# A searched order of 1,300 operations, searched again with GpSimd's casts kept apart from VectorE's on-chip operations

## The chip, the cores and the metric

The kernel runs on one core of one Trainium2 chip. The metric is the device time of one execution in microseconds. The inputs lie in HBM as float32 and the output goes there as float32. Inside, most operands are float16 and the sums in PSUM are float32.

## What is computed

The reference is a recurrence with decay for each head (B = 4 batches, H = 8 heads, S = 768 steps, D = 64), and then a mixer on its output, seen as 768 tokens by 512 channels for each batch:

```
gamma = 1.0 - 2.0 ** (-5.0 - np.arange(H))
scale = 1.0 / np.sqrt(D)
for t in range(S):
    state = gamma * state + einsum('bhd,bhe->bhde', k[:, :, t], v[:, :, t])
    y[:, :, t] = scale * einsum('bhd,bhde->bhe', q[:, :, t], state)
x = y.transpose(0, 2, 1, 3).reshape(B, S, H * D)

xt = x.transpose(0, 2, 1)
h  = maximum(xt @ w_tok1, 0) @ w_tok2        # 768 -> 256 -> 768 over the tokens
u  = x + h.transpose(0, 2, 1)
h2 = maximum(u @ w_ch1, 0) @ w_ch2           # 512 -> 1536 -> 512 over the channels
out = u + h2
```

## The kernel before

**The work and its stages.** The sequence is cut in six chunks of 128 steps. Two heads of 64 make a pair of 128 rows, so a batch has four pairs; "(2,1)" below is pair 1 of batch 2. `front(b, p)` is the work of one pair: 

- its k, q and v are loaded (`load`, L269). For batches 0 and 1 GpSimd's queue does that, and the transfer converts to float16 on its way; the very first k and all loads of batches 2 and 3 are issued on SP and arrive as float32 in tiles called `row` (L282).
- k is scaled by the decay of its step, one operation for each head (L343 on ScalarE or L345 on VectorE). For q the decay is either put in while its transpose is taken out of PSUM (L387, by the table `gq`), or with the same L343 and L345.
- where v came as float32, it is cast (L358 ScalarE, L360 VectorE or GpSimd). Six of those eight casts are GpSimd's, and besides issuing transfers and making two index tables at the start these are all that it does.
- k and q are turned so that a head's 64 dimensions lie on the partitions: by TensorE and a copy out of PSUM (L377, L379, L392), or, for batches 2 and 3 and some of batch 1, by a transposing transfer that SP issues (L367).
- "state matmuls" (L408) make each chunk's k times v; VectorE adds them up over the chunks with their decay (the chain of U, L418 and L420), and L434 or L436 writes them as the blocks of `diag`.
- "scores" (L453) are k times q inside a chunk, masked on VectorE (L463) into `am`. L474 and L483 give y from `am` with v and from `diag` with q.
- y is copied out as float16 `x` (L489), and the token mixer follows (L503 with its relu L512 or L514, and L523). Its result is cast to float16 `u` (L529) and copied to float32 `X` (L539), the sum onto which the channel mixer is added. u is turned too, on SP (L553) or on TensorE (L568, copied out at L575).

`back(b)` is the channel mixer of one batch: the widening 512 to 1536 (L606 with its relu L622; batches 2 and 3 use a scheme of seven products for eight, L679 to L725), and the narrowing 1536 to 512, also with seven products (operand sums L784, products L820 and L830, banks kept aside L810, additions to X L837, output L862). The last three blocks of batch 3 use plain products (L746, L755, L761). The schemes need sums and differences of weights, `wsum` (L904, L917), made once by VectorE.

**What sets the order.** Every operation is an `Op` in a list, with the engines that may do it. No planner runs in the kernel: a string, PLAN (L40 to L70), names the operations one by one in the order in which they are to be emitted. Two characters are an operation's number; one more says which engine does it, where there is a choice, and one more which of the eight PSUM banks it takes. A "+" with a digit stands for that many spare matmuls, zero times zero into bank 7, which keep TensorE from standing idle (L935, here called fillers). The loop that emits them:

```
    for step in placed(ops, PLAN):
        if isinstance(step, int):
            ...
            for _ in range(step):
                nc.tensor.matmul(spare[:, :384], zero[:, :P], zero, start=True, stop=True)
        else:
            step[1][3]()
```

Each engine, and each queue of transfers, takes its own instructions in that order and waits at each until what it reads is there and what it overwrites has been read. So an instruction whose input is late holds up all that stands behind it on its engine. Tiles of one name share a few buffers: `row` and `v` have four each, kT three, qT four, `diag` three, `am` six. A load into a buffer waits for the last reader of what the buffer held.

**The start.** Before the first pair, VectorE writes small tables: the logarithms of the decays `lgs` (L198 to L200), `lnh` (L219), the decay of a chunk `gp` (L229, L230), the mask, and zeros for `diag` (L233). From them ScalarE makes gk and gy (L204, L205), the scales of k and of q, and the table `gq` with four exponentials (L224). GpSimd issues the loads of batches 0 and 1 and of all weights, in one queue.

Of the kernel before, what the change touches and what calls it, by code (L numbers as in the profile page):

```python
# [39 lines left out]
PLAN = (  # L40
    "000b09010704020f0d1h00a031i10506+e1n0+31l11o1j20e1p081m1q0c1W31X1k0+31w121A1v451r1x1S0+42x30g1T1+21U41V0+42642"
    "1y0h0k1s2y1z0i2730292t11B51Y11t01Z1E61u02b2u00j201C281F2v21D0212w0+42H242a2c0222J232z32K1G02A240+12I212501H41I"
    "2L2d0m1J02f22g0l2B2M2C2e03812h02D2E390n0p2Q43413511N2i32F02G02j1K2k02N12O0r2P12l2R1L01O01M13630E2o3a72m03712T5"
    "2S02n01P00q2U3b2p03c3d3e2V03i033L61Q53k3f2q03g03j023l3h03n3m0u0o2W2X02Z0t3M2r33o20s3p2Y03013r00v3q03s4k13H13t0"
    "3I11R03u63v2s13w04l3273J53300x3x3A3N70w5s33y03D13B03F3z10z0yaC23C0aF03G13E0aDbc1bdbe5taEbf33O3K0bg3P3Qbl6bh311"
    "3R4g13S4h1aGbi2bmaHbn3V57413W3Y4m33Z0A3T04nbjaL0aMbk4i4aI2aNaJ4300F3X4074j04o3U1aK4u4156bA2410D0C0B4p444q4wbB"
    "4x4rbCb91b05b1421451b32ba4634P0b24Q14y474804v4T64V44cbJ3494a0bKb44s14Ubb4b0bL1d4W4X4R6b54YaU54S14C1aO7aP5o04d0"
    "aQbr3b624z6b74Z1f504t1b8bsaX74f4e14AaV4B0aR24DaS0G511aY521btaW535304aTaZbx21e4F74E154570Kby0I5p0bM4G4H0bu4bG5"
    "bvbo7bw565q04IbzbHbD25r0bNbO550H4J015bEbS0bQ31716bPbFbIbp0R5b55c602582bq59c8184Lcc7bR1bT5a05d04K05e45f5g1620"
    "4M04N01b631cd00L5Y0ce6bX0bY5Z0bV5hbW0c9cb5u15i065466bZch640J4O617M16A2cf67c005v5j07N0ci0685wcac4c1695x5k5yc25z"  # L50
    "5l0cl5m0cu5C10266a0N5Dcv5Ecy5cA4cj1cB0M6b0cm06C05A0cz1c5cq5F5H4cD5B05I6c0cE05Gcr6d62306gck5K75J05LcH5M05N36D0"
    "5O6hcn5P05Q5ncwcx0S0Q5R06f6l3c36ecI15TcF26m5U0cG5W6cM5X15V06EcN6y16i76j6z0dL6cJdq5cK5S1cocZ0dMdU27K16BdVdrcQ1"
    "dscRd84dNdW781cL19d96k1d00Pdk26F6790cS0OdR5dS6G6H6Id16n06JbU6K6o06p1ada1ccT46q0dO10T6L1dPcU6rdl7I17c0dQdT6s07b"
    "6t1d51dm7d16M07a2d6dw56N72066ud76Qdb16O6Rdcdd7J00VdX0dYdZ6P6v17edF76V18i1dn2dxdycV6W7O7f07g7P6dG6S56T8j0dHdo"
    "dh46U0di7hcg7icW77j6X07k6Y07Q7R6Z7Sdp7Ldz27l07008m1cpdjdAdB6w1cX717217T0U731cY74de2dfdg7n7340dt5du7U7p750d22d3"
    "7r7o8n06xdv760d47qdI07X75367v4e07s20X7V081e2e17m0dC18k2807YdD7t7wdJdE7W17u07x0dKeb67y1eIeJeK7Z1geceL7z850e470W"
    "7A08U00Ye507E7Be617C07F0e9cs18258o8S1eO3e38T0cCef837G07D0868Z2eg8l8W18p4ea0908qed7He79112840eM68818reP8s870e8"
    "89ee0ei8X18t92938a08e8ueh8beN08c08VeT177eU8d094ej8f0eRemeQes5eS0eteVen8x72438zeq5eo8h8Yc61eXeW09w08B11ct113er0"
    "8v08y9x00Z10a428AeYf0f19u2evew0f4epex7f5ey8w0ezf86cP08g0eueA0c708C18D970432989bf9eBfc8F08GeCfm28E0999aeD8I7f6"
    "fdcO08H0eEfa3fb8J950eFf7eZfnfo48K0961fffgfe78LfqfD5fh9c3fkfrfpfEa218M0ftfH9dfifAfja319y8N0fl9s19t19f49g9v149e0"  # L60
    "f219h08Ofu8P0fs68R9i18Q1fv9jfF79k0fy9lfGa90aa9z1fz9o9A9m0fIabfw9Bac9C9p09q0gm7fx9DadfKfJ2gnfR4fLgqfP9Eae9n0fS"
    "f319H0316fCfM9L9KfVfNfQg85fT69F0go1fO9Ja5grfWgtfX2fYgpfU9Ig9gs1gugcfZgvg09G0ge6ga0gbg5g39M3gAgdg6gfgy9Na60gggh"
    "9P09O09Qg1g2gwgxg79R0gkgigja709S29TgCfB9U0glgzg4gDgH19Y9VgI19W0gJ5gBgFgKgEaf0gZh34a89Z09X0gO7h0ah3526ajala1ai"
    "h40gMel09rh8gN0eH0gPh1akgQa01h90hcag0am3anha6ao0ap2gGhd1as0aqek0ar0gR1gSgVhbh2heathhau0avaw0hlgThmhfayhnh56az0"
    "hoh6h7hghp0hHax0hr3hw6hq0gWhxgLhuhZ1aBhshv0gUhAhL3i0ig7hyhIhMhti3hN5hihBgX0hz0hPhChKhDi4i6hOihhQhF0hJiki16ii5"
    "iu4hSi2ijidi7i56hR5ibhEhTilhUi8hXinhVicaA0hYiL0im1hWi9j55ioisipiaiviZ3ieiw2itiqiMirixiyizj17j0iN6iPgY0iBj3iQj4"
    "iIiOj2iR2iA6iSk67iCiDeG1jdiTj6j7iGjY1j8iJjbiXiUjeiHiEiYjcifjCj9jG4jEjajZk7k8iViFhj1hk1iWiKk0jfjgjN5k9jk2kahG0"
    "k1kbk2k3jDjOjRke6jH0jLjM0jijr3k4kckd1jPjFjl0jhjSk50jpjq0jI5jQ1jTjW1jsjJjtjvjjjKjwju0jm5jxjUjnjVjojykfkgkhjA0"
    "jX0kijzjB0kjkkkl0"
)  # L70


# [895 lines left out]
```

## Time and profile before

| | us |
|---|---|
| three runs | 188.21, 188.58, 189.45 |
| their median | 188.58 |
| the profiled execution: its own time | 188.52 |
| the profiled execution: its span, first to last instruction | 186.7 |
| VectorE busy | 167.7 |
| ScalarE busy | 122.1 |
| GpSimd busy | 33.6 |
| bytes moved | 30.23 MB |

The span is what the profile shows, and 188.52 - 186.7 = 1.82 us of the execution's time lie around it. Times inside the span are counted from its start. A row of a timeline reads: start, duration, engine, line, operation, output and input, shape, and how many like it follow in one go. Behind it, in brackets, stands how long the engine had been idle and whose result ended that. In a row that groups instructions, "x6 | 2.5, 415 | 0.9" means six of them, 2.5 us busy, 415 ns each on average, 0.9 us idle before them. "PE" is TensorE's matmuls, "DVE" VectorE, "ACT" ScalarE, "POOL" GpSimd, "SP" the engine that only issues transfers. The TensorE clock was granted in full in all 40 slices.

### The profile page before, as it was taken

Reading aid. Unit: us, or ns where it says so; the run is one execution under the profiler, and the core shown is the slowest. Engines: PE = TensorE matmul, PEld = TensorE weight load, DVE = VectorE, ACT = ScalarE, POOL = GpSimd, SP = SyncE. Lnnn points to the kernel's source line nnn. Section 1 sums busy time; section 2 is a strip of 40 time slices with the busy share of each in tenths; the row PEclk is TensorE's granted clock in tenths of the full one; section 3 lists DMA queues with packets and bytes.
Section 4 is the critical chain, followed back from the end, with each engine's and each line's share of the span. In section 5 each row is a group of like instructions: output and inputs, shape, how many; then the busy total and the mean of one; then the engine's idle time right before and its main releaser. Section 6 shows DMA issues by size and latency. Waiting matters only on the chain.

```text
span 186.7 us, 5207 instructions
## 1 busy us (share of the span) xinstructions
PE 178.8 (96%) x2075; PEld 134.9 (72%) x2075; DVE 167.7 (90%) x434; ACT 122.1 (65%) x279; POOL 33.6 (18%) x44
## 2 busy tenths in 40 slices
PE   7888999999999899999999999999999999999992
PEld 3445988677679779765768888776588986566782
DVE  3799998899999799889889999999999999879982
ACT  3837998856779676287988667689875254882110
POOL 8995676420001010001010000021000000000000
PEclk9999999999999999999999999999999999999999
DMA  8999999999999999999999959997926344011025
GB/s 113 154 171 195 178 176 178 185 187 205 190 183 217 183 230 167 148 226 205 131 228 234 162 101 215 312 192 171 157 42 146 111 140 185 2 58 58 32 112 197
DMA packets 94233, 30.23 MB, mean 162 GB/s; under 512 B 84352, under 2 KB 91264, under 8 KB 94208
## 3 DMA queue, kind: packets, MB, share of 16 engines
q1 hardware_dynamic: 61840, 17.63, 53.6%
q0 software_dynamic: 30208, 8.46, 43.8%
q10 hardware_dynamic: 2160, 3.80, 5.6%
q8 instruction: 16, 0.26, 0.6%
q14 instruction: 9, 0.07, 0.1%
HBM read 26.74 MB, written 6.29 MB: 177 GB/s over the span
## 4 chain that ended last, share of the span: by engine, by line
PE 59%; DVE 25%; DMA 6%; ACT 6%; issue 2%; POOL 0%; DVEq 0%; POOLq 0%; ACTq 0%
PE bank L606 15%; PE bank L820 9%; PE bank L679 9%; PE bank L830 7%; DVE am L463 5%; DVE X L837 4%; DMA row<-in_q_dram 4%; PE bank L503 4%; PE bank L523 3%; DVE U L420 3%; DVE hs L784 3%; PE bank L746 3%; DVE h L696 3%; DMA v<-in_v_dram 2%; PE bank L453 2%
## 5 line engine op out<-in xcount | busy, mean ns | idle before, releaser
L606 PE MATMUL bank<-uT,wc 128*128 128x384 f16 x192 | 36.4, 326 | 0.0
L463 DVE TENSOR_TENSOR am<-bank,mask 128x384 f16<-128x384 f32 x64 | 33.4, 552 | 1.5 <-PE bank L453 1.4
L622 ACT ACTIVATE h<-bank 128x384 f16<-128x384 f32 x48 | 22.0, 500 | 10.0 <-PE bank L606 9.8
L606 PEld LDWEIGHTS <-wc 128*128 128x128 f16 x192 | 17.3, 98 | 9.1 <-issue 0.2
L696 DVE TENSOR_TENSOR h<-bank,us 128x384 f16<-128x384 f32 x36 | 18.8, 553 | 2.0 <-ACT us L691 1.0
L691 ACT COPY us<-bank 128x384 f32<-128x384 f32 x36 | 16.6, 484 | 6.1 <-PE bank L679 2.2
L820 PEld LDWEIGHTS <-hs 128*128 128x128 f16 x198 | 18.8, 98 | 2.5
L810 ACT COPY us<-bank 128x256 f32<-128x256 f32 x26 | 9.6, 374 | 16.2 <-PE bank L820 13.8
L360 POOL CAST v<-row 128x768 f16<-128x768 f32 x6 | 5.0, 826 | 82.9 <-DMA row<-in_v_dram 53.6
L837 DVE TENSOR_TENSOR X<-X,bank 128x256 f32<-128x256 f32 x44 | 17.9, 417 | 1.0 <-PE bank L830 0.9
L420 DVE SCALAR_TENSOR_TENSOR U<-U,gp,bank 128x64 f32<-128x64 f32 x64 | 16.8, 278 | 0.8
L820 PE MATMUL bank<-wsum,hs 128*128 128x256 f16 x132 | 17.2, 273 | 0.0
L529 ACT CAST u<-bank 128x384 f16<-128x384 f32 x29 | 13.7, 491 | 4.1 <-PE bank L523 3.4
L679 PE MATMUL bank<-hs,wsum 128*128 128x384 f16 x72 | 15.1, 326 | 0.1
L434 ACT ACTIVATE diag<-U,gp 64x320 f16<-64x320 f32 x24 | 13.3, 559 | 2.6 <-DVE U L420 2.3
L523 PE MATMUL bank<-h,wt 128*128 128x128 f16 x192 | 14.8, 219 | 0.0
L489 ACT CAST x<-bank 128x384 f16<-128x384 f32 x27 | 12.2, 488 | 3.0 <-PE bank L483 2.9
L503 PE MATMUL bank<-x,wt 128*128 128x128 f16 x192 | 13.8, 219 | 0.2 <-DVE U L418 0.2
L830 PEld LDWEIGHTS <-h 128*128 128x128 f16 x132 | 12.5, 98 | 1.9
L679 PEld LDWEIGHTS <-wsum 128*128 128x128 f16 x96 | 9.1, 98 | 5.7 <-issue 0.4
L503 PEld LDWEIGHTS <-wt 128*128 128x128 f16 x192 | 11.9, 98 | 1.9 <-DMA wt<-in_moe_w_tok_dram 0.4
L523 PEld LDWEIGHTS <-wt 128*128 128x128 f16 x192 | 12.1, 98 | 1.2
(91 smaller groups left out, 364.4 us busy)
## 6 DMA issues: line engine op xcount, KB each, us to landing
out_dram<-X ACTq DMA_DIRECT2D x14, 256.0 KB, 2.3
row<-in_q_dram SPq DMA_DIRECT2D x8, 384.0 KB, 4.9
row<-in_v_dram SPq DMA_DIRECT2D x8, 384.0 KB, 5.1
row<-in_k_dram SPq DMA_DIRECT2D x8, 384.0 KB, 5.5
wc<-in_moe_w_ch_dram POOLq DMA_DIRECT2D x5, 512.0 KB, 13.3
out_dram<-X SPq DMA_DIRECT2D x9, 256.0 KB, 3.2
v<-in_v_dram POOLq DMA_DIRECT2D x8, 192.0 KB, 9.3
row<-in_q_dram POOLq DMA_DIRECT2D x8, 192.0 KB, 8.6
```

Source lines behind the costliest of these rows:

```text
L420: nc.vector.scalar_tensor_tensor(out=u[:, c], in0=u[:, c - 1], scalar=gp[:, p:p + 1], in1=st, op0=ALU.mult, op1=ALU.add)
L463: nc.vector.tensor_tensor(am, SC[g].tile[:, :m * P].rearrange("p (i t) -> p i t", t=P), mask.to_broadcast([P, m, P]), ALU.mult)
L503: nc.tensor.matmul(acc[:, jt * P:(jt + 1) * P], wt1[:, i, jt * P:(jt + 1) * P], X16.tile[:, i], start=(i + jt == 0), stop=(i == NC - 1), s ...
L523: nc.tensor.matmul(Y[hf].tile[:, i * P:(i + 1) * P], wt2[:, jt, t], H1.tile[:, jt], start=False, stop=(jt == NJ - 1), skip_group_check=True)
L606: nc.tensor.matmul(acc[:, :SH], wc1[:, ct, ft * P:(ft + 1) * P], UT.tile[:, ct, sh * SH:(sh + 1) * SH], start=(ct == 0), stop=(ct == NP - 1))
L622: nc.scalar.activation(H2.tile[:, ft], A.tile[:, :SH], AF.Relu)
L679: nc.tensor.matmul(acc[:, :SH], left(ct), r[:, ct], start=first and ct == 0, stop=ct == 1, skip_group_check=True)
L691: (nc.scalar.copy if e == "ACT" else nc.vector.tensor_copy)(kept(j), A.tile[:, :SH])
L696: nc.vector.tensor_tensor(into(hf)[:, ft], bank.tile[:, :SH], kept(j), ALU.add)
L820: nc.tensor.matmul(acc_[:, lo], l[:, j], r[:, j], start=first and j == 0, stop=j == K2 - 1, skip_group_check=True)
L830: nc.tensor.matmul(acc_[:, lo], l[:, j], r[:, j], start=first and j == 0, stop=j == K2 - 1, skip_group_check=True)
L837: (nc.vector if e == "DVE" else nc.gpsimd).tensor_tensor(dst(), dst(), b_(), ALU.add)
```

## The change

Only the table PLAN differs: another order, another choice of engine and of bank for the same operations, 38 fillers in place of 35. It comes out of a search that takes a cast on GpSimd and an on-chip operation of VectorE (one that reads and writes SBUF and no PSUM) to exclude each other, and that takes the time at which the early loads land from a trace. The first and last lines of the table:

```
 PLAN = (
-    "000b09010704020f0d1h00a031i10506+e1n0+31l11o1j20e1p081m1q0c1W31X1k0+31w121A1v451r1x1S0+42x30g1T1+21U41V0+42642"
...
+    "070504000b0102060f1h0031i108+g1n01j10d0a1o1p1q0e1l2+21W31k11m1v210h1S0091r1T01x1y0c1s+61B11U21X1w041A0g1V01Y5"
...
+    "jojX0kjjA0jzkkjB0kl0"
 )
```

What this does to the engines' own orders is shown at three places. The numbers behind a name (`k_115`, `bank_177`) only tell tiles apart.

At the start, ScalarE's order before. `us` is the buffer in which the first k, that of pair (0,0), lands:

```order
L204 ACT_TABLE_LOAD
L204 ACTIVATE gk<-lgs 128x8
L205 ACTIVATE gy<-lgs,lnsc 128x8
L343 ACTIVATE k_115<-us,gk 128x6x64
L224 ACTIVATE gq<-us,lnsc,lnh 128x384 x4
L392 COPY kT<-bank_177 128x768
L343 ACTIVATE k_233<-row,gk 128x6x64
L392 COPY kT<-bank_256 128x768
```

And now:

```order
L204 ACT_TABLE_LOAD
L204 ACTIVATE gk<-lgs 128x8
L205 ACTIVATE gy<-lgs,lnsc 128x8
L224 ACTIVATE gq<-us,lnsc,lnh 128x384 x4
L343 ACTIVATE k_124<-us,gk 128x6x64
L343 ACTIVATE k_215<-row,gk 128x6x64 x2
L392 COPY kT<-bank_240 128x768
L434 ACTIVATE diag<-U,gp 64x5x64 x2
```

The four exponentials go ahead of the first decay of k, the first copy of a turned k goes to VectorE, and both halves of the second pair's decay are ScalarE's.

SP's order where the loads of batch 2 begin, some 55 us into the execution, before:

```order
L553 DMA_TRANSPOSE uT<-u_1040 128x6x128
L282 DMA row<-in_q_dram 128x12x64
L282 DMA row<-in_v_dram 128x12x64
L282 DMA row<-in_k_dram 128x12x64
L282 DMA row<-in_q_dram 128x12x64 x2
L367 DMA_TRANSPOSE qT<-q_1317 128x6x128
L282 DMA row<-in_v_dram 128x12x64
L553 DMA_TRANSPOSE uT<-u_1229 128x6x128
L367 DMA_TRANSPOSE kT<-k_1327 128x6x128
```

And now:

```order
L553 DMA_TRANSPOSE uT<-u_1059 128x6x128
L282 DMA row<-in_v_dram 128x12x64
L282 DMA row<-in_k_dram 128x12x64
L282 DMA row<-in_q_dram 128x12x64
L282 DMA row<-in_v_dram 128x12x64
L282 DMA row<-in_q_dram 128x12x64
L282 DMA row<-in_k_dram 128x12x64
L367 DMA_TRANSPOSE kT<-k_1262 128x6x128
L367 DMA_TRANSPOSE qT<-q_1324 128x6x128
```

The first three loads are those of pair (2,0), q, v, k before and v, k, q now. The two q behind them were those of (2,3) and (2,1); now v, q and k of (2,1) follow, and q of (2,3) comes later.

VectorE's order at the same place, before. `q_1317` is q of pair (2,0), `q_1405` that of (2,3):

```order
L345 TENSOR_SCALAR q_1317<-row,gy 128x6x64
L837 TENSOR_TENSOR X<-X,bank_1336 128x256
L784 TENSOR_TENSOR hs<-hs,h_814 128x768
L784 TENSOR_TENSOR hs<-h_814,hs 128x768
L418 COPY U<-bank_1373 128x64
L345 TENSOR_SCALAR q_1405<-row,gy 128x6x64
L837 TENSOR_TENSOR X<-X,bank_1329 128x256
L420 SCALAR_TENSOR_TENSOR U<-U,gp,bank_1373 128x64
L418 COPY U<-bank_1360 128x64
```

And now, where `k_1262` is k of pair (2,0), in row 111 of VectorE's order:

```order
L904 TENSOR_TENSOR wsum<-wc_81 128x1536
L784 TENSOR_TENSOR hs<-hs,h_798 128x768
L784 TENSOR_TENSOR hs<-h_798 128x768
L345 TENSOR_SCALAR k_1262<-row,gk 128x6x64
L837 TENSOR_TENSOR X<-X,bank_1300 128x256
L784 TENSOR_TENSOR hs<-h_798,hs 128x768
L784 TENSOR_TENSOR hs<-h_821 128x768
L418 COPY U<-bank_1330 128x64
L418 COPY U<-bank_1341 128x64
```

One half of the k of (2,0) now stands ahead of the U copies, and no q does.

Over the whole execution these instructions change engine. ScalarE: L343 from 23 to 25, L358 from 1 to 2, L392 from 6 to 4, L434 from 24 to 25, L489 from 27 to 30, L512 from 15 to 14, L529 from 29 to 27, L539 from 22 to 25, L575 from 3 to none, L810 from 26 to 29, its output transfers (L862) from 13 to 11. VectorE: L345 from 25 to 23, L360 from 1 to none, L392 from 2 to 4, L436 from 8 to 7, L489 from 5 to 2, L514 from 1 to 2, L529 from 3 to 5, L539 from 10 to 7, L575 from 3 to 6, L810 from 7 to 4. GpSimd keeps six casts, with the v of pair (2,3) in place of that of (2,1).

More of the change, by code (lines that the diff above doesn't have):

```diff
@@ L40 @@
 PLAN = (
[L41 to L69, printed above, removed]
+    "070504000b0102060f1h0031i108+g1n01j10d0a1o1p1q0e1l2+21W31k11m1v210h1S0091r1T01x1y0c1s+61B11U21X1w041A0g1V01Y5"
+    "1Z+126231t02021274629221z1u0+71E02t02b1C1F2a280i0j2x62u02z32v4232A2y2B2C2D2E2f20k2w0+42H641D02401G02502K2J"
@@ new lines @@
+    "+23850m1H32F02c42d1I392G11J02N62g2I351K0l2L2M2e02h01N1L02i32O2j0n1M02Q11O02k00p3413511P00q2R3652l2m03a02P1371"
+    "3i533b2o2S03c3d3e3l0E2n02p02T72U2q03f3k0u3L43j233m2V02Z2W3n1Q53H13g03h03o23p0o1R12X03003r33s3112Y12r73253q00r"
+    "0s2s13313t00t0x3I03u03v5s63w05t3N73x0v3y03A3B03z03J53K0aF03M3D63FaC23E13C0aDaG0A3G1bc6aE3Obd3V2354aHbe3P3Q4g1"
+    "4k04h1bf64lbi1bgbjbh3R3S3ZbkaL00w3Y4i6bl4bm4j13WaM3XbG5bH4u26174xbn4m34w4n4340z3T0bIb953U04o0y4vba401bD64p4144"
+    "bbbJ5420aI2bEaNbF450aU0bKaVaX64q1b4rbL4s11f4P04y0F4t14Q11daR3aSaT46747aW4T34800C0D4V0aY49aJaZ4a04R74W4U4XaK5o0"
@@ new lines @@
+    "6t0dC30OdDdrds0N6ubU7M17N16v1cJcKdL1dEcodMdA6w1dN7c07d0dB0S6N25346R6P6F66GcQ17edb7cRd25dk0dw46Od3dxdy6H6I6Q7a2"
+    "6V3dldR2cScp6JcZ40V6K781d51d6d06L06S6d4dm6M16T7911adS6Wd1dU46U06X0dc6Y0dT6Z7K2d77P27010T7Q7f10W7gcT5cL7R7S7h71"
+    "7207bcU7Odt0730ddducV7i74751dn68i17j1gdh7do8j17TdvdpcW0cXcY7Ld85de6d98m07617kda7U8S1dfdidjdg7n52137r0Ye08T17o"
+    "7q7pe40e1dF6dGdHdVdWe507V0e3e20UdX3dI70XdY7X14657Z8l817l1dJe9dZea08n08odO37s2dPe647Y11dQ7W0dKe7edeb37m0eI7v4"
+    "eM77t7w8218W0ee0ei7u07y56x7x0eJeLecef83eN07zeK1c80cCej8VcP1eRemeg8X18U0850en868407A08k27BeS08Z38p5908q7E8708r"
@@ new lines @@
+    "gygga60ge6gwg3g1a70ghgxg2gAgkgigBgjg7gC9S7gDg6gF9R09Taf0gEa8ek1gG9U0glgH1ag09V9YgJ48R9W0gKgI0g4gzgZh37h409Z0"
+    "a009X0gO0gPgMah5436h0aigN0h52gSgQakgR0h8alajam4h1gLap69rh2gTanaqgVh91hlhnao0ar0a1as3athcau0avayh6aw0hd1h7hmgW"
+    "gUax0az0hw2ha3hbhxhp1hq1hr4hshhhehihohHhL4hAaBhthIhJhfhMhuhv0ig7hN0hghOhBhyhz0hZ3hCi15hPhDi0hQi3aA1hShF1gY1gX0"
+    "hR2ihikii6i2hKhTi4hXi6ilinj15hUijhVhWhEhYi7iu4i56iL0i8iw2ivioim1iyizixipisi9iqiairidiBiMiZ2iN6j0ibiCiA1j3iOic"
+    "iIiPj4iDiQj53iEiGiSiteG1iHk67iR6iJj2iTiFiUj6j7k7iXiVjbjY4j8iYhk0jcjZk0ieiKjejdifjCk1j9k2k3iWjajEjfjgjhjDjG3jH0"
@@ L70 @@
+    "jk6jl0jN2jOjik8k9kakbkckd1hG1jLjM0hj0jr0jFk4jPjRjQ0jsjSjpjI4jTjUjW1jq0jtk50jJjjjKjVjvjm3ju0jyke4kfjwjxkgjnkhki"
+    "jojX0kjjA0jzkkjB0kl0"
 )
```

10 lines of the change are left out of this document (added).

## The prediction

> **What bounds the kernel now.** I read the page's busy time and slices first, then the chain that ended last, and then the timelines of TensorE and VectorE at the places where that chain leaves TensorE.
>
> ```profile
> span 186.7 us, 5207 instructions
> PE 178.8 (96%) x2075; PEld 134.9 (72%) x2075; DVE 167.7 (90%) x434; ACT 122.1 (65%) x279; POOL 33.6 (18%) x44
> PE   7888999999999899999999999999999999999992
> DVE  3799998899999799889889999999999999879982
> PE 59%; DVE 25%; DMA 6%; ACT 6%; issue 2%; POOL 0%; DVEq 0%; POOLq 0%; ACTq 0%
> ```
>
> TensorE is at nine tenths or more from slice 5 on, but for one slice of eight tenths, and VectorE is nearly as full. The matmuls are the same before and after, except for three more fillers (L935). So a new order can only remove what TensorE waits. The sum is made against this execution: 186.7 us of span plus 1.82 us around it, 188.52 us, which is 0.06 under the median of the runs, 188.58.
>
> The chain leaves TensorE for long at the start, around 55 to 65 us, around 84 us and from 95 to 133 us. These rows of TensorE's timeline show three waits in the middle:
>
> ```profile
> 63.93 0.82 PE L820 MATMUL bank<-wsum,hs 128*128 128x256 f16 x6
> 65.44 0.51 PE L453 MATMUL bank<-qT,kT 64*128 64x128 f16 x12 [0.69 <-DVE U L420]
> 65.88 0.83 PE L820 MATMUL bank<-wc,h 128*128 128x256 f16 x6
> 66.54 0.82 PE L830 MATMUL bank<-wc,h 128*128 128x256 f16 x6
> 69.34 0.28 PE L483 MATMUL bank<-diag,qT 128*128 128x128 f16 x2
> 69.90 0.51 PE L453 MATMUL bank<-qT,kT 64*128 64x128 f16 x12 [0.28 <-PE bank L483]
> 83.84 1.46 PE L606 MATMUL bank<-uT,wc 128*128 128x384 f16 x8
> 85.67 0.51 PE L453 MATMUL bank<-qT,kT 64*128 64x128 f16 x12 [0.37 <-DVE X L539]
> ```
>
> Undisturbed, six L820 hold the engine 0.66 us from start to start (65.88 to 66.54), so the scores at 65.44 start 65.44 - 63.93 - 0.66 = 0.85 late. Two L483 take some 0.12, so those at 69.90 are 69.90 - 69.34 - 0.12 = 0.44 late. At 85.67 the named wait alone is 0.37; eight L606 at 0.163 each make it 0.53. Sum of the three: 1.8 us.
>
> **Part 1: the casts and VectorE.** The change keeps GpSimd's casts of v (L360) away from VectorE's operations that read and write SBUF alone. Two of the six casts fell beside one:
>
> ```profile
> 66.17 0.83 POOL L360 CAST v<-row 128x768 f16<-128x768 f32 x1 [7.47 <-DMA row<-in_v_dram]
> 84.12 0.83 POOL L360 CAST v<-row 128x768 f16<-128x768 f32 x1 [17.13 <-PE bank L523]
> ```
> ```profile
> 66.42 0.98 DVE L784 TENSOR_TENSOR hs<-hs,h 128x768 f16<-128x768 f16 x1
> 84.11 1.04 DVE L345 TENSOR_SCALAR k<-row,gk 128x384 f16<-128x384 f32 x1
> 85.08 0.54 DVE L539 COPY X<-bank 128x384 f32<-128x384 f32 x1
> ```
> ```profile
> L345 DVE TENSOR_SCALAR q<-row,gy 128x384 f16<-128x384 f32 x6 | 2.5, 415 | 0.9 <-DMA row<-in_q_dram 0.9
> L784 DVE TENSOR_TENSOR hs<-h 128x768 f16<-128x768 f16 x18 | 10.0, 554 | 0.9 <-ACT h L622 0.5 <-issue 0.2 <-PE bank L820 0.2
> ```
>
> The same forms take 0.554 and 0.415 elsewhere, so the two lost 0.43 and 0.63, 1.06 us together. Not all of it is on the path. The copy at 85.08 follows the held one directly, and the scores at 85.67 waited for it: without the 0.63 their 0.53 goes. The 0.43 at 66.42 lies inside the lateness of 69.90 and is counted in part 2. Gain of part 1 alone: 0.5 us, between 0 (if the copy's place is taken by something else that is late) and 1.06.
>
> The Trainium skill, "SBUF — State Buffer", section "SBUF: two separate sides", says that VectorE and GpSimd share one pair of ports by an exclusive lock, taken by a VectorE operation of a two-port mode or with two SBUF inputs, and that the one that comes second waits fully. The lengthened rows agree with it. By the same section GpSimd's writing of DMA descriptors contends too, which no cast rule shuts out; that is the last rival below.
>
> **Part 2: the loads of batch 2.** They are issued on SP, and the chain of waits has one of them:
>
> ```profile
> 55.08 7.13 DMA row<-in_q_dram
> ```
> ```profile
> 61.07 0.22 DVE L418 COPY U<-bank 128x64 f32<-128x64 f32 x1
> 62.23 0.42 DVE L345 TENSOR_SCALAR q<-row,gy 128x384 f16<-128x384 f32 x1 [0.94 <-DMA row<-in_q_dram]
> ```
> ```profile
> 57.88 0.82 POOL L360 CAST v<-row 128x768 f16<-128x768 f32 x1 [19.16 <-DMA row<-in_v_dram]
> ```
> ```profile
> 59.52 1.12 ACT L343 ACTIVATE k<-row,gk 128x384 f16<-128x384 f32 x2 [0.25 <-DMA row<-in_k_dram]
> ```
>
> VectorE stood 0.94 us for the q of pair (2,3), whose scores come some 30 us later; the chains of U, and so the scores at 65.44 and 69.90, stood behind it. The new order has no q there: that load stands 15th in SP's order in place of 6th, and its scaling far behind. The stop goes. What is late next is the k of pair (2,0). In the old SP order the loads are q, v, k; v was in by 57.88 and k by 59.52, so the third came some 1.7 us behind the second. The new order is v, k, q, so k takes the second place and lands near 57.8. VectorE's k decay (row 111 of its new order) stands ahead of the U copies of two pairs. By counting the DVE rows ahead of it, VectorE gets there near 56.4, and waits 1.4 us instead of 0.94. TensorE gets to the state matmuls of (2,0) near 57.8 (before at 60.5; there is about 1.8 us less of its work ahead of them, the rest from parts 1 and 3 and from smaller waits). Their operands are ready when ScalarE's half of the decay is, 57.8 + 0.62, so TensorE waits some 0.65. Before, the same place and the two score waits cost 0.25 + 0.85 + 0.44 = 1.54 (0.25 is the small gap behind the state matmuls at 60.5). Gain: 1.54 - 0.65 = 0.9 us, between -1 (k one load later, see the rivals) and 1.5.
>
> The transposing DMAs of k and q of (2,0) have less room than before: kT and qT stand some 2.5 to 3 us of TensorE work ahead of their scores in the new order, before 6.7. kT can be issued near 59 and qT near 61; behind the loads of pair (2,1) they land at about 65.5, and the scores come at about 66.8. No cost, with 1.3 us in hand.
>
> **Part 3: the start.** The first state matmuls waited for v and nothing else; now they wait for ScalarE, because gq (four exponentials) goes ahead of its decay of k.
>
> ```profile
> 4.51 0.61 ACT L343 ACTIVATE k<-us,gk 128x384 f16<-128x384 f32 x1 [2.08 <-DMA us<-in_k_dram]
> 5.14 0.82 DVE L219 MEMSET lnh<- 64x1 f32 x8
> 5.42 2.50 ACT L224 ACTIVATE gq<-us,lnsc,lnh 128x384 f32<-128x384 f32 x4 [0.29 <-DVE lnh L219]
> 6.04 0.46 PE L408 MATMUL bank<-v,k 128*64 128x64 f16 x10 [0.26 <-DMA v<-in_v_dram]
> ```
>
> VectorE now sets gp, lnh and lgs in this order, about 2.0 us from 1.1 on, so gk and gy are there at 3.5, gq at 3.5 + 2.5 = 6.0, the decay at 6.7, and TensorE's first work starts 0.66 later. In return gq is done 1.9 us earlier, VectorE copies the first kT itself, v of pair (0,1) is asked for two loads earlier, and both decays of (0,1) and (0,2) are on ScalarE. I chained the two orders by the durations of their rows and kept the landings at their old spacing of 1.1 to 1.4 us a load. The second scores of pair (0,3) then start near 25.1 instead of at 25.60 (row below), but with the six transposes of u of (0,0) (0.34 us) still to do: 0.2 us gained. Between -0.7 and +0.7, since that chain has some twenty links. The three added fillers (38 against 35) lie in this stretch and are in the 0.2; were they not covered, they would cost 3 x 0.163 = 0.5.
>
> ```profile
> 25.16 0.51 PE L568 MATMUL bank<-ident,u 128*128 128x128 f16 x6
> 25.60 0.34 PE L453 MATMUL bank<-qT,kT 64*128 64x128 f16 x6
> ```
>
> **Part 4: work moved between engines.** VectorE has 5 instructions less (net), ScalarE 7 more without its output DMAs, of which two go to SP. Most that move are copies and casts of a bank at 0.55 us on VectorE and 0.37 to 0.49 on ScalarE:
>
> ```profile
> L539 DVE COPY X<-bank 128x384 f32<-128x384 f32 x10 | 5.5, 552 | 0.5 <-ACT u L529 0.5
> L489 DVE CAST x<-bank 128x384 f16<-128x384 f32 x5 | 2.7, 553 | 0.2 <-PE bank L483 0.2
> L810 DVE COPY us<-bank 128x256 f32<-128x256 f32 x7 | 2.8, 419 | 0.5 <-PE bank L820 0.5
> L575 DVE COPY uT<-bank 128x768 f16<-128x768 f16 x2 | 1.1, 552 | 0.0
> ```
>
> Off VectorE go three each of these first three, two L345, one L360 and one L436; onto it three L575, two L392, two L529 and one L514. By their row means that is 2.4 us less busy, about 2.0 less of the engine (consecutive ones overlap by 0.085). It is worth nothing by itself while TensorE is the bound; it is what lets VectorE follow when TensorE comes earlier, in the stretch from 95 to 133 us where the chain runs along VectorE. There VectorE must come earlier by as much as TensorE does: parts 1 to 3 need 1.6, and VectorE has 1.06 from the casts plus 1.6 of the relief that lies ahead of 95 us, less the 0.4 longer wait for k: 2.2. So nothing is given back. ScalarE is 65% busy, and 0.9 us more of it hides there.
>
> **The tail** is the same: the last rows of TensorE are the last blocks' L820, L830 and L746, VectorE adds, ScalarE issues the last output. Zero, between -0.2 and +0.3 (a sixth L746 pair now stands in the last group).
>
> **Sum.** 188.52 - 0.5 - 0.9 - 0.2 = 186.9. My own chains are off by half a microsecond and more, about the length of a cast (0.83), so I let one of the six meet such an operation after all and count half of its mean loss of 0.53: 0.3 us. Forecast 187.2 us; its own range is 186.3 to 188.2.
>
> **Rivals.**
>
> *Slower: k of (2,0) lands one load later.* Place: the k decay on VectorE, row 111. Old loads landed 1.7 us apart, but the fourth only at 62.21 (55.08 + 7.13), 2.7 behind the third. If v, k and q share the rate, so that k is in with the third or fourth and lands at 61.2, VectorE stands 61.2 - 56.4 = 4.8 us, and TensorE, which comes to the state matmuls at 57.8, waits 61.2 + 0.62 - 57.8 = 4.0 instead of 0.65: 187.2 + 3.4 = 190.6. It decides from a landing of about 59.5 (188.9). Against it: the load before k was in by 57.88 in second place. 0.14.
>
> *Faster: all of VectorE's relief comes through.* VectorE is the chain from 97 to 133 us; if it reaches 95 us earlier by the full 1.06 + 1.6 and TensorE's small waits there go too, the end is 2.66 earlier: 185.9. For it: DVE at nine tenths in slices 21 to 34. Against it: TensorE too is at nine tenths there, and it must have gained as much by then. 0.25.
>
> *No change: the locks stay.* The casts drift beside other operations, or the descriptors do what the casts did. These rows bear it out:
>
> ```profile
> 3.99 1.03 POOL L295 DMA_DIRECT2D row<-in_k_dram  x1
> 10.92 1.12 POOL L295 DMA_DIRECT2D row<-in_k_dram  x1
> ```
> ```profile
> 4.52 0.67 DVE L345 TENSOR_SCALAR k<-us,gk 128x384 f16<-128x384 f32 x1 [1.64 <-DMA us<-in_k_dram]
> 11.27 0.85 DVE L345 TENSOR_SCALAR k<-row,gk 128x384 f16<-128x384 f16 x1
> ```
>
> Beside descriptor writing VectorE lost 0.67 - 0.42 and, against the 0.31 of the shortest of this form, 0.85 - 0.31: 0.8 us. Two casts and as much again beside descriptors, 1.06, would return part 1 and the half of part 2: 188.3. 0.20.
>
> **Chances and range.** Forecast 0.41, the three rivals 0.14, 0.25 and 0.20. A measurement of this kernel can tell about 1% from no change, here 186.69 and 190.47. Faster: 0.25 and a small part of the forecast's own range, 0.30. Slower: most of the first rival, 0.13. The same: 0.57. The range goes from 185.7, just under the faster rival, to 189.3, the slower rival's case with k at 59.5 and some more; outside it are the worst of that rival and the tails, 2 in 10.
>
> **What would show it.** Right: no stop of VectorE for a q of batch 2 near 62; no L784 or L345 above 0.6 us beside a cast; TensorE's first L408 at 6.7 and its second L453 of pair (0,3) near 25; a wait of TensorE under 1 us at the state matmuls of (2,0). Wrong: VectorE standing over 2 us for a k of batch 2, TensorE waiting for kT or qT of (2,0), or new waits of TensorE between 95 and 133 us.

## The result

The changed kernel takes 189.35 us (median of 12 runs, 188.81 to 190.22), the kernel before in the same runs 188.34 (187.83 to 189.45). The ratio is 1.0055 with a 95% interval of 1.0034 to 1.0077, so it is about 1.0 us slower. The forecast was 187.2 with a range up to 189.3: the time lies just above the range, on the other side of no change.

The profiled execution took 188.81 us, the quickest of the twelve. From the page: the span, busy time, two rows of slices, the chain's shares.

```profile
span 187.0 us, 5213 instructions
PE 178.5 (95%) x2078; PEld 134.9 (72%) x2078; DVE 165.9 (89%) x429; ACT 123.9 (66%) x284; POOL 34.7 (19%) x44
PE   7699999999999999999999999989999999999992
DVE  4799999898899999896999999978999999789882
PE 78%; DVE 12%; DMA 4%; issue 2%; ACT 2%; POOLq 1%; POOL 0%; DVEq 0%
```

VectorE lost 1.8 us of busy time and the chain's share on it fell from 25% to 12%, as the change wanted. The hole in the middle (slice 13, 61 to 65 us) is gone, and a new one is in the slice of 122 to 126 us. TensorE's timeline shows both. The three score groups that waited 1.8 us together before:

```profile
63.48 0.51 PE L453 MATMUL bank<-qT,kT 64*128 64x128 f16 x12
67.93 0.51 PE L453 MATMUL bank<-qT,kT 64*128 64x128 f16 x12
79.97 0.51 PE L453 MATMUL bank<-qT,kT 64*128 64x128 f16 x12
```

They stand without a wait now. Two new stops of TensorE:

```profile
56.78 0.82 PE L830 MATMUL bank<-wc,h 128*128 128x256 f16 x6
58.02 0.83 PE L820 MATMUL bank<-wsum,hs 128*128 128x256 f16 x6 [0.43 <-DVE hs L784]
...
125.17 0.49 PE L679 MATMUL bank<-uT,wc 128*128 128x384 f16 x2
126.12 0.35 PE L408 MATMUL bank<-v,k 128*64 128x64 f16 x10 [0.47 <-POOL v L360]
126.89 0.35 PE L408 MATMUL bank<-v,k 128*64 128x64 f16 x10 [0.43 <-POOL v L360]
```

Reckoned from start to start as in the prediction, the L820 is 58.02 - 56.78 - 0.66 = 0.58 late. The state matmuls of pair (3,3) are 126.12 - 125.17 - 0.33 = 0.62 late and those of (3,2) another 126.89 - 126.12 - 0.28 = 0.49: 1.1 us at 126 us. The kernel before has both groups there in one go, without such a stop:

```profile
126.21 0.50 PE L523 MATMUL bank<-h,wt 128*128 128x128 f16 x6
126.64 0.51 PE L408 MATMUL bank<-v,k 128*64 128x64 f16 x20
```

**Behind the first stop** is a collision of the kind that the change was to shut out. GpSimd and VectorE in the changed kernel:

```profile
55.05 1.63 POOL L360 CAST v<-row 128x768 f16<-128x768 f32 x1 [15.20 <-DMA row<-in_v_dram]
83.83 0.83 POOL L360 CAST v<-row 128x768 f16<-128x768 f32 x1 [3.23 <-DMA row<-in_v_dram]
97.71 1.18 POOL L360 CAST v<-row 128x768 f16<-128x768 f32 x1 [13.05 <-DMA row<-in_v_dram]
```
```profile
55.05 0.95 DVE L904 TENSOR_TENSOR wsum<-wc,wsum 128x1536 f16<-128x1536 f16 x1
55.92 1.58 DVE L904 TENSOR_TENSOR wsum<-wc 128x1536 f16<-128x1536 f16 x1
57.42 0.55 DVE L784 TENSOR_TENSOR hs<-hs,h 128x768 f16<-128x768 f16 x1
...
58.36 0.41 DVE L345 TENSOR_SCALAR k<-row,gk 128x384 f16<-128x384 f32 x1
...
84.13 0.73 DVE L345 TENSOR_SCALAR k<-row,gk 128x384 f16<-128x384 f32 x1
```

The cast of v of pair (2,0) starts when v lands, in the middle of four L904. It takes 1.63 us in place of 0.83 beside one of them, and the next L904 takes 1.58 in place of 0.95; then the operand sum L784 is late, and TensorE's L820 with it. The cast at 83.83 meets an L345 (0.73 in place of 0.42), and the one at 97.71 takes longer itself; neither stops TensorE here. That agrees with the section of the Trainium skill that the prediction cites ("SBUF — State Buffer", "SBUF: two separate sides"): whoever comes first keeps the ports for the whole instruction, in both directions.

**Behind the second stop** is the order of two loads. The chain of waits and SP's and GpSimd's timelines:

```profile
116.93 8.16 DMA row<-in_v_dram
```
```profile
116.23 2.14 SPq L282 DMA_DIRECT2D row<-in_v_dram  x2
```
```profile
125.24 1.60 POOL L360 CAST v<-row 128x768 f16<-128x768 f32 x2 [26.36 <-DMA row<-in_v_dram]
```

SP asks for v of (3,2) first and of (3,3) second; the second lands at 116.93 + 8.16 = 125.09. GpSimd's order has the cast of (3,3) first, and TensorE's state matmuls are in that order too. So the cast of (3,3) starts at 125.24 and the other stands behind it, though its v had landed at 122.40 by the trace. Before, the order of the casts was that of the loads:

```profile
123.07 0.83 POOL L360 CAST v<-row 128x768 f16<-128x768 f32 x1 [27.02 <-DMA row<-in_v_dram]
125.75 0.83 POOL L360 CAST v<-row 128x768 f16<-128x768 f32 x1 [1.86 <-PE bank L503]
```

The later v landed at much the same time there, at 125.61. TensorE reached the place about 1 us later (126.21 + 0.33 against 125.17 + 0.33) and found both casts all but done. So the 0.62 of pair (3,3) is a load that came no earlier while TensorE did, and the 0.49 of pair (3,2) is the order.

### The profile page after: what moved, and what is told of

Its sections match the earlier page's. It is cut to its first block, busy times and chain, and to the rows that moved or that the text cites. A ratio compares the mean times of both kernels' runs of the same rounds, so it can differ in the third digit from the quotient of the medians.

```text
span 187.0 us, 5213 instructions
## 1 busy us (share of the span) xinstructions
PE 178.5 (95%) x2078; PEld 134.9 (72%) x2078; DVE 165.9 (89%) x429; ACT 123.9 (66%) x284; POOL 34.7 (19%) x44
## 4 chain that ended last, share of the span: by engine, by line
PE 78%; DVE 12%; DMA 4%; issue 2%; ACT 2%; POOLq 1%; POOL 0%; DVEq 0%
PE bank L606 16%; PE bank L820 15%; PE bank L679 12%; PE bank L830 11%; PE bank L523 5%; DMA row<-in_v_dram 4%; PE bank L503 4%; PE bank L453 4%; DVE am L463 3%; PE bank L746 3%; DVE wsum L904 2%; PE bank L474 2%; PE bank L408 2%; PE bank L483 2%; DVE qT L387 1%
## 5 line engine op out<-in xcount | busy, mean ns | idle before, releaser
L463 DVE TENSOR_TENSOR am<-bank,mask 128x384 f16<-128x384 f32 x64 | 32.9, 551 | 1.5 <-PE bank L453 1.4
L696 DVE TENSOR_TENSOR h<-bank,us 128x384 f16<-128x384 f32 x36 | 19.2, 553 | 3.2 <-PE bank L679 1.1
L810 ACT COPY us<-bank 128x256 f32<-128x256 f32 x29 | 11.0, 380 | 16.6 <-PE bank L820 14.9
L360 POOL CAST v<-row 128x768 f16<-128x768 f32 x6 | 6.1, 1020 | 80.9 <-DMA row<-in_v_dram 57.8
L820 PEld LDWEIGHTS <-hs 128*128 128x128 f16 x198 | 18.6, 98 | 3.3 <-DVE hs L784 0.7
L837 DVE TENSOR_TENSOR X<-X,bank 128x256 f32<-128x256 f32 x44 | 18.1, 417 | 2.5 <-PE bank L830 1.8
L529 ACT CAST u<-bank 128x384 f16<-128x384 f32 x27 | 12.8, 488 | 8.9 <-PE bank L523 8.7
L820 PE MATMUL bank<-wsum,hs 128*128 128x256 f16 x132 | 17.9, 273 | 0.4 <-DVE hs L784 0.4
L679 PE MATMUL bank<-hs,wsum 128*128 128x384 f16 x72 | 15.5, 326 | 0.0
L489 ACT CAST x<-bank 128x384 f16<-128x384 f32 x30 | 13.7, 485 | 1.3 <-PE bank L483 1.0
L434 ACT ACTIVATE diag<-U,gp 64x320 f16<-64x320 f32 x25 | 14.0, 562 | 0.3
L679 PEld LDWEIGHTS <-wsum 128*128 128x128 f16 x96 | 9.0, 98 | 5.2 <-issue 0.3
```

The source lines that it names most:

```text
L463: nc.vector.tensor_tensor(am, SC[g].tile[:, :m * P].rearrange("p (i t) -> p i t", t=P), mask.to_broadcast([P, m, P]), ALU.mult)
L679: nc.tensor.matmul(acc[:, :SH], left(ct), r[:, ct], start=first and ct == 0, stop=ct == 1, skip_group_check=True)
L696: nc.vector.tensor_tensor(into(hf)[:, ft], bank.tile[:, :SH], kept(j), ALU.add)
L820: nc.tensor.matmul(acc_[:, lo], l[:, j], r[:, j], start=first and j == 0, stop=j == K2 - 1, skip_group_check=True)
L837: (nc.vector if e == "DVE" else nc.gpsimd).tensor_tensor(dst(), dst(), b_(), ALU.add)
```

## The experiments

Theory A: the middle gained what was forecast, and the loss is new waits, above all the one at 126 us. Rival B: another engine, VectorE first, is as late as TensorE there, so that taking a wait away only moves it. All experiments change nothing but the order of operations or the engine of a cast, except where the edit says more. Each ratio is to the kernel before, run beside it. In diffs, a name in brackets is the pair.

### Both kernels once more

> The changed kernel once more, for a second profiled execution and more times beside those of the kernel before. Theory A (the gain of the middle is lost at the last two v): 189.3 us, 1.0 over the kernel before; the profile shows TensorE waiting about 1 us in all at the state matmuls of pairs (3,3) and (3,2) near 126 us, and TensorE ahead of the kernel before from 65 to 120 us. Rival B (the time is lost at the start or at the cast near 55 us, and the wait at 126 us only takes slack): the waits at 126 us change from one execution to the next, and the end with the start.

189.03 us, ratio 1.0042 (1.0020 to 1.0065). The second execution (189.71 us):

```profile
127.06 0.35 PE L408 MATMUL bank<-v,k 128*64 128x64 f16 x10 [0.95 <-POOL v L360]
127.84 0.35 PE L408 MATMUL bank<-v,k 128*64 128x64 f16 x10 [0.43 <-POOL v L360]
```
```profile
97.59 1.20 DVE L784 TENSOR_TENSOR hs<-h 128x768 f16<-128x768 f16 x1
```
```profile
99.32 0.81 PE L830 MATMUL bank<-wc,h 128*128 128x256 f16 x6 [0.42 <-DVE am L463]
```

The stop at 126 us is there again and longer (the group ahead starts at 125.63, so 1.1 and 0.5). Here the cast at 97.6 us held VectorE as well (1.20 in place of 0.55) and TensorE stood some 0.6 at 99 us. So a stop that one execution shows may be missing in the next; the collision at 55 us and the double cast at 126 us are in both.

> The kernel before once more, for a second profiled execution. Both theories: 188.4 us, TensorE's three waits at 65.4, 69.9 and 85.7 us as before (1.8 us together, give or take 0.3), and no wait of TensorE for a v near 126 us.

188.28 us, ratio 1.0006 (0.9987 to 1.0026). The same three places of TensorE now lose 0.36, 0.54 and 0.13 (scores at 65.06, 69.65 and 85.02 us): 1.0 together, not 1.8. At 85 us there is next to nothing: the cast at 84.29 came behind the scaling of k this time (0.40 at 83.87), and an L345 at 84.88 took only 0.45. The prediction read all three from one execution. Against the expectation, the kernel before lost some 0.3 us on a v too: its L408 at 126.35 take 0.82 together in place of 0.51, and the cast of (3,2) ends at 126.78.

### The order of the last two v

```diff
 GpSimd, its last two casts
-L360 CAST v (3,3)
-L360 CAST v (3,2)
+L360 CAST v (3,2)
+L360 CAST v (3,3)
 TensorE, with VectorE's U chains in the same way
-L408 (3,3); L408 (3,2); L679; L523
+L408 (3,2); L679; L523; L408 (3,3)
```

> GpSimd casts v of pair (3,2), which lands first, ahead of that of (3,3); TensorE's state matmuls and VectorE's U chains of the two pairs change places in the same way, the second after two more groups of matmuls. Theory A: the waits of 0.6 and 0.5 us of TensorE at 126 us go, and the whole is 1.1 us shorter than the changed kernel, 188.25 us, no slower than the kernel before. Rival B: the end is set by something else behind 126 us (VectorE, or loads of q and k of batch 3), and the time stays within 0.3 of the changed kernel, 189.05 to 189.65.

188.77 us, ratio 1.0018 (1.0000 to 1.0036), against 1.0042 of the changed kernel beside it: 0.3 us won by the medians, 0.5 by the ratios, with intervals of some 0.4 us each way, and not 1.1. Its timelines of GpSimd, TensorE and VectorE:

```profile
123.11 0.83 POOL L360 CAST v<-row 128x768 f16<-128x768 f32 x1 [23.59 <-DMA row<-in_v_dram]
125.87 0.83 POOL L360 CAST v<-row 128x768 f16<-128x768 f32 x1 [1.93 <-DMA row<-in_v_dram]
```
```profile
126.41 0.35 PE L408 MATMUL bank<-v,k 128*64 128x64 f16 x10
130.26 0.80 PE L453 MATMUL bank<-qT,kT 64*128 64x128 f16 x12
131.20 0.49 PE L679 MATMUL bank<-hs,wc 128*128 128x384 f16 x2
```
```profile
130.60 0.55 DVE L696 TENSOR_TENSOR h<-bank,us 128x384 f16<-128x384 f32 x1
```

The cast of (3,2) is done at 123.94 in place of 126.84, and the stop at 126 us is down to 0.2. But now the scores at 130.26 take 0.80 in place of 0.51 and L679 at 131.20 starts 0.5 late in all: it follows an L696 of VectorE that ends at 131.15. The time falls between the two theories: some of the stop was worth its length at the end, and the rest only moved.

The next edit keeps TensorE's order and moves the loads; GpSimd's two casts are exchanged as above.

```diff
 SP, from the load of q of (3,2) on
 L282 DMA row q (3,2)
+L282 DMA row v (3,2)
+L282 DMA row k (3,2)
 L553 DMA_TRANSPOSE uT x3
-L282 DMA row k (3,2)
+L282 DMA row v (3,3)
 L862 DMA out x2
-L282 DMA row v (3,2)
-L282 DMA row v (3,3)
```

> The changed kernel with the last two loads of v issued earlier on SP: that of pair (3,2) and its k right behind q of (3,2), ahead of three transposes of u, that of (3,3) ahead of two outputs; GpSimd casts (3,2) first. TensorE's and VectorE's orders stay. Theory A (the loss at 126 us is the lateness of the last v): both casts are done before 124 us, no wait at the state matmuls of (3,3) and (3,2), and 1.1 to 1.6 us shorter than the changed kernel: 187.6 to 188.1, a little faster than the kernel before. Rival B (behind the wait VectorE is as late as TensorE, so that removing it only moves the wait, as in the run with the exchanged order): 0.2 to 0.6 shorter, 188.6 to 189.0.

191.5 us, ratio 1.0178 (1.0150 to 1.0205): a miss of both. TensorE, VectorE and SP:

```profile
118.91 0.48 PE L679 MATMUL bank<-uT,wc 128*128 128x384 f16 x2 [2.46 <-DVE X L837]
129.49 0.51 PE L408 MATMUL bank<-v,k 128*64 128x64 f16 x20
```
```profile
117.63 0.56 DVE L647 TENSOR_TENSOR hs<-uT 128x768 f16<-128x768 f16 x1 [2.65 <-DMA uT<-u]
118.11 0.74 DVE L837 TENSOR_TENSOR X<-X,bank 128x256 f32<-128x256 f32 x2
```
```profile
109.31 3.12 SPq L282 DMA_DIRECT2D row<-in_k_dram  x1
112.47 5.36 SPq L553 DMA_TRANSPOSE uT<-u  x3
```

Both v were cast by 123.2 us and the state matmuls are back to one group with no wait, which fits that the stop was the late v, though TensorE comes 3 us later here. But three loads behind one another kept SP busy (the third took 3.12 to issue), the transposes of u began at 112.47 in place of 107.83, and the uT landed at 117.6 to 120.2. VectorE works in its order: its sum L647 waited 2.65 us for the first uT, the L837 behind it ended at 118.85, and TensorE's L679, which needs the bank that L837 frees, stood 2.46. Moving the last loads of v ahead of these transposes cost more than the stop that it took away.

### GpSimd's last instructions

Both executions of the changed kernel take about 0.35 us more than the kernel before from TensorE's last matmul to the end. In the quickest one, that of the result, this is all of the difference: VectorE's last addition is even a little earlier than before (second row, changed) and the span 0.3 us longer.

```profile
183.46 0.42 DVE L755 TENSOR_TENSOR X<-X,bank 128x256 f32<-128x256 f32 x1 [0.51 <-PE bank L746]
183.38 0.42 DVE L755 TENSOR_TENSOR X<-X,bank 128x256 f32<-128x256 f32 x1 [0.28 <-PE bank L746]
```

The busy rows do not show what follows; GpSimd's own records behind the last transfer do (the start of its clearing of semaphores, of the drain ahead of it, the time between them, and the count of its records):

```
kernel            records   drain    clear   stand
before                 75   186.14   186.27   0.13
before, again          75   186.17   186.30   0.13
changed                72   186.09   186.58   0.49
changed, again         72   186.99   187.46   0.47
one cast fewer         70   186.60   186.73   0.13, and 0.45 two records later
four fills more        76   185.94   186.06   0.12
```

"One cast fewer" is the run with the cast of (2,0) on ScalarE, below. In all with 70 to 72 records, GpSimd stands some 0.36 us longer than elsewhere ahead of its 69th record, with no work left to do. With 75 or 76, the 69th falls in the idle stretch before the closing.

```diff
         step[1][3]()
+    pad = const_p.tile([P, 1], FP, name="pad")
+    for _ in range(4):
+        nc.gpsimd.memset(pad, 0.0)
```

> The changed kernel with four more one-column fills on GpSimd behind its last cast, where GpSimd is idle until the end. The records of all runs so far show that behind the last transfer GpSimd stands 0.34 us before the 69th of its recorded instructions; in the kernel before, which has 75 of them, that one lies in an idle stretch, in the changed one, which has 72, in the closing sequence. Theory A (part of the loss is this stand at the very end): 0.34 shorter than the changed kernel, 188.8, with GpSimd's clearing of the semaphores right behind the drain. Rival B (the stand has another cause and stays): no change, 189.2.

188.75 us, ratio 0.9997 (0.9972 to 1.0022). The stand is gone (last row above). The ratio fell by 0.0045 to 0.0058, some 0.9 us, with an interval of half a microsecond each way, so the run says that there is a gain and the records say how much: 0.36.

> The changed kernel with the exchanged order of the last two v and the four fills of GpSimd together. If both gains add up (0.3 to 0.6 from the first by its own run, 0.34 from the second): 188.3 to 188.6, level with the kernel before. Rival B: as the exchanged order alone, 188.8.

188.34 us, ratio 0.9996 (0.9973 to 1.0018): level with the kernel before, as expected. But the fills alone had 0.9997, so on top of them the exchanged order shows no gain; with half a microsecond each way, 0.3 to 0.5 could hide in that.

### The collision at 55 us

```diff
 GpSimd, its first cast
-L360 CAST v (2,0)
 ScalarE, behind two u casts
-L622 h; L539 COPY X
+L358 CAST v (2,0)
 L343 k (2,0); L512
+L622 h
 L810
+L539 COPY X
```

> In the changed kernel the cast of v of pair (2,0) goes from GpSimd, where it took 1.63 us beside two L904 of VectorE, to ScalarE behind its u casts. Theory A: VectorE's L904 takes 0.96 instead of 1.58, TensorE's wait of 0.6 at 58 us goes, but what it gains is lost again at 126 us: the end within 0.2 of the changed kernel (189.15 to 189.55), with a wait at 126 us longer by 0.6. Rival B (the loss near 55 us is what the end shows): 0.6 shorter, 188.75.

190.03 us, ratio 1.0105 (1.0078 to 1.0132), a miss. L904 takes 0.95 as it should, but ScalarE's copy came late, and with it a bank:

```profile
59.15 0.51 PE L408 MATMUL bank<-v,k 128*64 128x64 f16 x20 [1.26 <-ACT X L539]
```

This edit made its own wait and tells nothing of the end. The next leaves the cast where it is and moves what it holds up, VectorE's fourth L904: behind one L784 (on top of the early loads), behind three operations, and behind four, the last an L837.

```diff
 VectorE
 L904 wsum
-L904 wsum
 L784 hs
+L904 wsum, first run
 L784 hs; L345 k (2,0)
+L904 wsum, second run
 L837 X
+L904 wsum, third run
```

> The kernel with early loads, and VectorE's fourth L904 goes behind the operand sum L784 that TensorE waits for at 58 us. Both theories: that wait of 0.59 goes. Theory A: another 0.6 shorter than the run with early loads alone, 187.0 to 187.5. Rival B: no more than 0.2 shorter.

192.25 us, ratio 1.0211 (1.0179 to 1.0243); the wait at 58 us is gone, one of 0.69 at 59.5 us has its place.

> The changed kernel with VectorE's fourth L904, the one that the cast of v of pair (2,0) holds up, moved behind three short operations: both L784 and the scaling of k of pair (2,0), so that what TensorE waits for at 58 and at 59.5 us comes ahead of it. Theory A (the collision near 55 us costs the end what it costs TensorE there): no wait of 0.59 at 58 us and none at 59.5, and 0.5 to 0.6 shorter than the changed kernel, 188.6. Rival B (VectorE is behind anyway, and the time is taken back until 126 us, where TensorE waits longer for the same v): within 0.2, 189.0 to 189.4.

189.65 us, ratio 1.0067 (1.0039 to 1.0095). Again:

```profile
59.30 0.35 PE L408 MATMUL bank<-v,k 128*64 128x64 f16 x10 [0.62 <-DVE X L837]
```

The bank of the state matmuls of (2,0) comes free with VectorE's L837, which stood behind the moved L904.

> As the run before with L904 moved, and one place further: behind the addition L837 too, which frees the bank that the state matmuls of pair (2,0) waited for at 59.3 us. Theory A: no wait of TensorE over 0.2 us between 57 and 62 us, and 0.5 to 0.6 shorter than the changed kernel, 188.6. Rival B (taken back until 126 us, or drowned by the spread of the executions): 189.0 to 189.4.

188.81 us, ratio 1.0015 (0.9991 to 1.0039). With L837 ahead, there is still a collision (the third L904 takes 1.58 at 55.72) but TensorE does not feel it:

```profile
58.10 0.82 PE L820 MATMUL bank<-wsum,hs 128*128 128x256 f16 x6
58.84 0.51 PE L408 MATMUL bank<-v,k 128*64 128x64 f16 x20
59.28 0.51 PE L523 MATMUL bank<-h,wt 128*128 128x128 f16 x6
```

Against 1.0042 to 1.0055 of the changed kernel that is 0.5 to 0.8 us less, each way about as uncertain as that: it agrees with the 0.58 that TensorE waits for the collision. The profiled execution, one of the slowest of its runs (189.90), stood 1.6 us at 126 us.

> The same move of L904, the exchanged order of the last two v, and GpSimd's four fills behind its last cast, together. Theory A: 0.5 below the run with the last two alone, 187.8, faster than the kernel before. Rival B: 188.2 to 188.4.

188.65 us, ratio 1.0017 (0.9996 to 1.0038); it holds the second place of L904, which only moved the wait.

> The same, with the exchanged order of the last two v and GpSimd's four fills. Theory A: 187.8, faster than the kernel before. Rival B: 188.3 to 188.6, level with it.

188.10 us, ratio 0.9985 (0.9967 to 1.0004), between the two theories. The three repairs take the changed kernel from 1.0 us behind the kernel before to 0.3 ahead, not clear of no change. Together they won 1.2 us, and the move of L904 only 0.2 on top of the other two (0.9996). One by one they had shown 0.3 to 0.7, 0.9 and 0.5 to 0.8, which adds up to more: single differences of half a microsecond are at the limit of what these runs can tell.

### The start

```diff
 TensorE, near 13 us
-L935 fillers x7
+L935 fillers x4
```

> The changed kernel with 35 fillers, as before, in place of 38: the group of seven near 13 us becomes four. By the prediction they are covered: no change (189.0 to 189.4). Theory that the start is 0.2 us late because of them: up to 0.49 shorter, 188.7.

189.18 us, ratio 1.0047 (1.0024 to 1.0069): no change. The next matmuls wait 0.66 for VectorE's mask in place of 0.17.

```diff
 ScalarE
-L224 gq x4
 L343 k (0,0)
+L224 gq x4
```

> The changed kernel with ScalarE's half of the first decay of k ahead of the four exponentials, as in the kernel before. TensorE's first state matmuls start at 6.0 instead of 6.7. Theory A (behind them the landings of q and VectorE's chain set the start): TensorE's second scores of pair (0,3) stay within 0.2 of 25.6 and the end within 0.2 of the changed kernel, 189.0 to 189.4. Rival B (the first decay sets the start): 0.5 shorter, 188.7.

189.52 us, ratio 1.0066 (1.0034 to 1.0097): no gain. Its TensorE:

```profile
5.71 0.35 PE L408 MATMUL bank<-v,k 128*64 128x64 f16 x10
7.79 0.53 PE L377 MATMUL bank<-ident,row 128*64 128x128 f16 x12 [1.30 <-DMA row<-in_q_dram]
25.72 0.34 PE L453 MATMUL bank<-qT,kT 64*128 64x128 f16 x6
```

The first work starts 1 us earlier and then waits 1.3 for q.

### The parts of the prediction, alone, on the kernel before

```diff
 VectorE
-L345 q (2,3)
 L837; L420 and L418 of both U chains; L784; L837
+L345 q (2,3)
```

> The kernel before with VectorE's half of the scaling of q of pair (2,3) moved behind the U chains of the two pairs: the stop of 0.94 us near 62 us alone, as in part 2 of the prediction, without the new order of the loads. By the prediction TensorE's scores at 65.4 and 69.9 us come 0.9 earlier and the end with them: 187.5. Theory A: the lead is kept until 126 us, where the state matmuls then wait for the last v as long as the lead: 188.1 to 188.4. Rival B (VectorE bounds 95 to 133 us): the lead is lost before 126 us already, 188.1 to 188.4, with no wait for a v.

187.46 us, ratio 0.9961 (0.9930 to 0.9991): 0.88 faster by the medians (0.2 to 1.3 by the interval of the ratio), the fastest of all kernels here. VectorE's stop near 62 us is gone (the q follows at 64.36), and TensorE's scores:

```profile
64.71 0.51 PE L453 MATMUL bank<-qT,kT 64*128 64x128 f16 x12
68.85 0.51 PE L453 MATMUL bank<-qT,kT 64*128 64x128 f16 x12
```

They come 0.7 and 1.05 earlier than in the first execution, and the end follows. Little takes it back: at 126 us TensorE waits 0.4, for a copy L539 of VectorE and not for a v.

```diff
 GpSimd
-L360 CAST v (2,1); L360 CAST v (2,2)
 ScalarE, behind L434 near 69 us and L622 near 85 us
+L358 CAST v (2,1); L358 CAST v (2,2)
```

> The kernel before with the two casts that met VectorE's on-chip operations (pairs (2,1) and (2,2), at 66 and 84 us) on ScalarE: part 1 of the prediction alone. By the prediction 0.5 us shorter than the kernel before, 187.85. By theory A the operations of VectorE at 66 and 84 us take 0.55 and 0.41 and the scores near 85.7 come 0.5 earlier, but at 126 us the state matmuls wait for the last v as much longer: 188.3, no change.

188.91 us, ratio 1.0029 (1.0011 to 1.0046): slower. The operations of VectorE are short and the scores of 85.67 come at 84.75, but ScalarE's relu is late behind the cast and TensorE loses most of that again:

```profile
84.75 0.51 PE L453 MATMUL bank<-qT,kT 64*128 64x128 f16 x12
85.19 0.51 PE L523 MATMUL bank<-h,wt 128*128 128x128 f16 x6
86.36 0.81 PE L606 MATMUL bank<-uT,wc 128*128 128x384 f16 x4 [0.66 <-ACT h L622]
```

And this kernel too has 72 records on GpSimd and the stand of 0.47 at its end, which is most of the 0.5 that it lost. The run is outside both expectations and does not price the collisions: that they cost nothing does not follow.

## Why the prediction was wrong

The step that failed is "nothing is given back" in part 4: the last two v took back 1.1 to 1.6 us of TensorE. Two smaller ones are part 1's premise that the casts would meet nothing (0.6) and a tail put at zero (0.36). The prediction's own sign of being wrong, new waits of TensorE between 95 and 133 us, came at 126 us.

**Part 2, the loads of batch 2, had the right stop.** It gave 0.9 for the stop at the q of pair (2,3) and what stood behind it; the stop alone measured 0.88. That they agree so well is partly luck: the 0.9 was 1.54 less a wait of 0.65 for k of (2,0), the run has the old loads and no such wait, and of the 1.54 the second execution of the kernel before had less to win. In the changed kernel VectorE did not wait for k of (2,0) at all: k came with the second load, as the prediction chose (it landed at 56.70, not 57.8), and VectorE reached its decay at 58.36, not 56.4; the collision accounts for some 0.6 of that. The slower rival, k one load later, did not happen.

**Part 1, the casts, was wrong in its premise.** It took the exclusion at its word. In the traces of the changed kernel and its variants the cast at 55 us, where GpSimd does it, met L904 or a sum L784 in every execution profiled; that at 84 us met an L345 in every one too (0.53 to 1.03 in place of 0.42), that at 97 us a sum in some. The search excludes them in its own times; in the traces the cast at 55 us starts between 1.8 and 3.3 us behind VectorE's first L904, and moves with its load. The no-change rival had this mechanism ("the casts drift beside other operations") and a chance of 0.20, but at a price of 1.06 for two casts returned, to 188.3. The collision at 55 us stands ahead of what TensorE needs next, stops it for 0.58 and costs about that by the repair alone. And the 0.5 gained at 85.67 was read from one execution; the second had 0.13 there without any change.

**Part 3, the start,** gave 0.2 and got none: first state matmuls at 6.70 as forecast, second scores of (0,3) at 25.58 in place of the 25.1 forecast. With the six transposes still to do (0.34), as the prediction reckons it, that is 0.3 behind the kernel before and not 0.2 ahead; 0.2 of it is made up in the next 10 us. The three fillers are covered, as it said.

**Part 4 failed at "nothing is given back".** It compared VectorE's relief with TensorE's lead from 95 to 133 us, and did not follow GpSimd's order there. The last two casts stand against the order of their loads, and the later load comes no earlier than before: 1.1 to 1.6 us of TensorE at 126 us. Mending the order brought back 0.3 to 0.5, while VectorE is late for the rest. It also counted ScalarE 7 instructions more; the pages have 284 against 279, and 1.8 us more busy, not 0.9, which cost nothing that a run shows.

**The tail** was put at zero and costs 0.36, in GpSimd's closing instructions.

The sum by measured parts: -0.9 (part 2), +0.6 (collision at 55 us), +0.3 to +0.5 (order of the last v), +0.36 (end) makes +0.4 to +0.6; measured are +0.8 to +1.0. What is left, 0.2 to 0.6, is not settled by the runs: the wait at 99 us that some executions have (0.6) and the missing part of the middle, where the second execution of the kernel before had less to win (1.0) than the first (1.8), are both large enough.

The traces say where the lead went. Take the scores of a pair as marks, and allow for matmuls that stand on the other side of a mark by their usual time from start to start (an estimate, to some 0.1 us). Against the first execution of the kernel before, TensorE in the two executions of the changed kernel is 0.1 and 0.1 us behind at the scores of (1,2), 0.9 and 0.9 ahead at those of (2,1), 0.9 and 0.4 ahead at (3,1), and 0.1 and 1.05 behind at (3,2). So the middle did win 1.0, collision included, and the stretch of the last two v took it all back, and more in the second. That place levelled the kernel before too: its second execution was 0.55 ahead of its first at (3,1) and level at (3,2), with its last v landing at 125.80 against 125.61. In the run with the scaling of q moved, the last v landed at 123.86, and the lead stayed.
